# Triangular solves of a chunked delta rule: the substitution left to one engine, two groups interleaved, blocks moved by transfers

## The chip, the cores and the metric

The kernel runs on one NeuronCore of a Trainium2 chip. The metric is the device time of one execution in microseconds (us), taken as the median of several runs. Five engines work in parallel, each in its own program order: PE (TensorE: matrix products, with PEld for its weight loads), DVE (VectorE), ACT (ScalarE), POOL (GpSimd) and SP (SyncE, which here only issues transfers). Engines wait for each other by semaphores. SBUF is the on-chip memory of 128 rows, and PSUM takes the products of TensorE.

## The reference

Three parts follow each other. The first is a linear attention with a delta rule, for 4 batches, 8 heads, 768 tokens and head size 48; the other two are a gated block and a mixer block of dense products.

```python
k_n = k / (norm(k) + 1e-6)
for t in range(S):
    y[t]  = q[t] @ state
    v_old = state.T @ k_n[t]
    state = state + beta[t] * outer(k_n[t], v[t] - v_old)
# then
h = gelu(x @ w_in); u, v = halves of h; v = layernorm(v)*g_ln
x = x + (u * (w_sg @ v + b_sg)) @ w_out
u = x + (relu(x.T @ w_tok1) @ w_tok2).T
out = u + relu(u @ w_ch1) @ w_ch2
```

The change concerns the first part alone.

## The kernel before

The attention goes over six groups, g = 0 to 5. A group is two batches by 256 tokens, and holds four steps c = 0 to 3 of 64 tokens each, for all eight heads. Inside 64 tokens the recurrence is replaced by the inverse T of a triangular matrix, which is worked out per group ahead of time, so that the recurrence over the tokens becomes a recurrence over c.

The preparation of one group (`prep`, `qk`) has these parts:

- kk: the products K K^T (line 141 on TensorE), four blocks per group in a PSUM tile `gm`. ScalarE moves each block out in pieces of 32 rows: four copies to `Md` (line 145, the 32 by 32 diagonal blocks) and two to `G` (line 146, the blocks below them).
- pre: VectorE transposes `Md` to `Li` (line 151), works out the norms and scales `Li` (lines 158 to 170).
- solve: 31 steps of forward substitution on 128 rows at once (128 rows by 8 problems each). Step j takes a product `p` (line 191) and adds it to `T` (line 193). The columns of T are cut into three sets: columns 0 to 3 and 4 to 10 or 11 go to VectorE, and the rest to GpSimd; each set has its own `p`.
- post: four transposes of 32 rows (line 197) put T^T in its place in `tw`, the operand of the chain, and one of 128 rows (line 201) makes `Tn`.
- merge and wt: products on TensorE (lines 209, 218, 229) join two 32-token blocks to one of 64 and multiply with K; ScalarE takes each out of PSUM (lines 212, 221, 232).
- qk: the products Q K^T (line 121), four blocks per group. VectorE multiplies each by a triangular mask into `aq` (line 128), two instructions per block; for group 0 ScalarE copies and GpSimd masks.
- V: GpSimd scales all of V by the norms (line 91), and ScalarE copies it to its place in `yr` for each c (line 238, `vput`).

The recurrence of a group (`chain`) is a generator of 16 slots, four per c: `u` (products ck, line 270, and four copies, line 272), `d0` (products Sps, line 256, and copies, line 258; V of the next c), `y0` and `y1` (output products, line 246). Between the slots a table, `act`, lists what of the preparation of groups g+1 and g+2 is issued there: K a block of kk, Q one of qk, S n steps of the solve, m a merge, w a wt, l and v the loading and placing of V. In the last slots of `chain` of group 5 the dense part begins (`tail`).

The order of the work is written out by hand: there is no scheduler, each engine runs its instructions in the order in which the Python code issues them, and a transfer stands in the order of the engine that issues it. `warm(n)` issues n products on a tile of zeros (line 300, into `wm`), whose results nobody reads. Beside the chains of groups 1 and 2 `beside` converts a weight (lines 413 to 418 on VectorE, 389 and 391 on GpSimd, its transfers on SP).

## Time and profile before

| | |
|---|---|
| median of 3 runs | 1005.87 us (1003.7 to 1007.04) |
| span of the profiled execution | 1010.4 us |
| PE busy | 889.8 us (88%) |
| DVE busy | 660.8 us (65%) |
| ACT busy | 425.5 us (42%) |
| POOL busy | 317.1 us (31%) |

The page gives the span of the profiled execution, from its first to its last instruction, and no other time for it; it lies 4.5 us above the median of the runs. A row of a timeline gives start, duration, engine, line, operation, output and inputs, shape and count; brackets hold how long the engine sat idle before and who ended that. A row of the windows gives a stretch of the span, its length, the busy time of each engine with its instructions, the clock that TensorE was granted as a share of full speed, and the load of the transfer engines. The six chains begin, by their first ck products, at 71, 132, 191.7, 243.8, 290.9 and 325.9 us; the dense part is alone from about 372 us.

### The profile page before, as it was taken

The numbers are of one execution on the slowest core, as the hardware profiler recorded it, in microseconds if no ns is written. First come the engines' busy times: TensorE is split into PE (matmuls) and PEld (weight loads), VectorE is DVE, ScalarE is ACT, GpSimd is POOL, SyncE is SP. The second block draws the span as 40 slices with busy tenths as digits, with TensorE's granted clock in tenths as the row PEclk, the third lists the DMA queues.
The fourth block names the chain that finished last, engine by engine and source line by source line (L and its number), as shares of the span: only waits on it lengthen the run. The fifth ranks groups of instructions, "written<-read, shape, count | busy, mean of one in ns | idle before, by whom it ended". The sixth has DMA issues, their size and how long they took to land.

```text
span 1010.4 us, 23691 instructions
## 1 busy us (share of the span) xinstructions
PE 889.8 (88%) x9764; PEld 819.7 (81%) x9764; DVE 660.8 (65%) x1612; ACT 425.5 (42%) x1029; POOL 317.1 (31%) x475
## 2 busy tenths in 40 slices
PE   6376787777869889999999997988899999999998
PEld 4164666656757678999999996888899999999998
DVE  5999999999993578884956897878623123123122
ACT  6265675666857864442333423334312112112111
POOL 4474446627261234423423453744300000000000
PEclk8688998888999999999999998989999999999999
DMA  9320254715131332000000022223200000000000
GB/s 371 130 49 1 69 127 159 180 57 121 35 75 38 139 125 64 1 1 1 1 2 1 1 72 66 94 63 111 67 24 25 1 24 24 1 24 24 1 25 23
DMA packets 28955, 60.99 MB, mean 60 GB/s; under 512 B 3760, under 2 KB 9904, under 8 KB 28080
## 3 DMA queue, kind: packets, MB, share of 16 engines
q1 hardware_dynamic: 28848, 59.49, 19.1%
q8 instruction: 76, 1.25, 0.5%
q14 instruction: 31, 0.25, 0.1%
HBM read 51.61 MB, written 7.86 MB: 59 GB/s over the span
## 4 chain that ended last, share of the span: by engine, by line
PE 59%; DVE 28%; ACT 7%; issue 4%; POOL 1%; DVEq 0%; POOLq 0%; ACTq 0%
PE ps L489 18%; PE ps L490 18%; PE ps L491 18%; DVE p L191 6%; DVE T L193 6%; DVE tw L197 3%; DVE F L413 2%; DVE aq L128 2%; DVE F L414 2%; PE wm L300 1%; PE ps L513 1%; DVE F L415 1%; DVE F L418 1%; ACT Md L145 1%; DVE Li L151 1%
## 5 line engine op out<-in xcount | busy, mean ns | idle before, releaser
L581 DVE SCALAR_TENSOR_TENSOR hlo<-ps,hh 128x384 fp32r<-128x384 f32 x96 | 53.5, 557 | 208.9 <-ACT hh L580 208.9
L580 ACT ACTIVATE hh<-ps 128x384 fp32r<-128x384 f32 x96 | 47.2, 492 | 229.8 <-PE ps L491 229.8
L489 PE MATMUL ps<-GU,SB 128*128 128x384 f32 x288 | 98.7, 343 | 0.0
L491 PE MATMUL ps<-GU,SB 128*128 128x384 f32 x288 | 98.4, 342 | 0.0
L490 PE MATMUL ps<-GU,SB 128*128 128x384 f32 x288 | 98.1, 341 | 0.0
L191 DVE TENSOR_TENSOR p<-Li,T 128x31 f32<-128x31 f32 (+28 forms) x348 | 87.7, 285 | 1.1
L193 DVE TENSOR_TENSOR T<-T,p 128x31 f32<-128x31 f32 (+28 forms) x348 | 84.1, 274 | 0.8
L490 PE MATMUL ps<-SB,VHt 128*128 128x384 f32 x192 | 65.8, 343 | 2.3 <-POOL SB L391 2.3
L491 PE MATMUL ps<-VHt,hlo 128*128 128x384 f32 x192 | 65.3, 340 | 1.3 <-DVE hlo L581 1.3
L300 PE MATMUL wm<-dum 128*128 128x512 bf16 x156 | 51.5, 436 | 16.4 <-DVE dum L319 14.8
L489 PE MATMUL ps<-SB,VHt 128*128 128x384 f32 x192 | 65.6, 341 | 0.0
L491 PE MATMUL ps<-SB,VHt 128*128 128x384 f32 x192 | 65.2, 339 | 0.0
L489 PE MATMUL ps<-VHt,hh 128*128 128x384 f32 x192 | 65.0, 338 | 0.0
L490 PE MATMUL ps<-VHt,hh 128*128 128x384 f32 x192 | 64.6, 337 | 0.0
L556 POOL TENSOR_TENSOR q<-q,u 128x384 f32<-128x384 f32 x32 | 36.9, 1159 | 66.5 <-DVE q L555 66.5
L489 PE MATMUL ps<-X,SA 128*128 128x384 f32 x144 | 50.0, 347 | 7.2 <-DVE xn L568 3.2
L490 PEld LDWEIGHTS ps<-GU,SB 128*128 128x128 f32 x288 | 54.9, 191 | 0.6 <-DVE GU L506 0.6
L489 PEld LDWEIGHTS ps<-GU,SB 128*128 128x128 f32 x288 | 55.0, 191 | 0.5 <-DVE GU L506 0.5
L491 PEld LDWEIGHTS ps<-GU,SB 128*128 128x128 f32 x288 | 54.8, 190 | 0.3 <-POOL SB L391 0.3
L191 POOL TENSOR_TENSOR p<-Li,T 128x19 f32<-128x19 f32 (+19 forms) x115 | 41.4, 360 | 35.2 <-DVE T L168 27.1
L229 PE MATMUL gm<-tw,kn 128*48 128x64 f32 x768 | 30.2, 245 | 23.9 <-DVE aq L128 19.7
L490 PE MATMUL ps<-X,SA 128*128 128x384 f32 x144 | 49.3, 343 | 0.0
(153 smaller groups left out, 2429.7 us busy)
## 6 DMA issues: line engine op xcount, KB each, us to landing
st<-in_ch_dram SPq DMA_DIRECT2D x36, 256.0 KB, 2.9
kq<-in_kq_dram SPq DMA_DIRECT2D x16, 544.0 KB, 6.8
v<-in_vn_dram SPq DMA_DIRECT2D x12, 384.0 KB, 4.2
out_dram<-xn SPq DMA_DIRECT2D x24, 192.0 KB, 1.9
aq<-in_qt_dram SPq DMA_DIRECT2D x4, 1024.0 KB, 14.9
aq<-in_qt_dram SPq DMA_DIRECT2D x8, 512.0 KB, 7.7
kn<-in_kn_dram SPq DMA_DIRECT2D x2, 1536.0 KB, 17.2
st<-in_win_dram SPq DMA_DIRECT2D x12, 256.0 KB, 4.7
```

The source lines that it names most:

```text
L128: else: nc.vector.tensor_tensor(aq[rr,par].rearrange("p a c x -> p (a c) x"),gp[rr],mask[rr].rearrange("p t x -> p (t x)").unsqueeze(1).to ...
L191: e.tensor_tensor(p,Li[:,j,j+1:].unsqueeze(1).to_broadcast([128,w,n]),T[:,a:a+w,j].unsqueeze(2).to_broadcast([128,w,n]),ALU.mult)
L193: e.tensor_tensor(T[:,a:a+w,j+1:],T[:,a:a+w,j+1:],p,ALU.add)
L197: nc.vector.transpose(out=tw[rr,q//2,:,co:co+32].rearrange("p n i -> p i n"),in_=T[rr].rearrange("p c i -> p i c"))
L229: nc.tensor.matmul(wt[D_[par],2*pair+cc,:],KNs[pb][F_[par],bb,par,2*h+cc,pair,:],tw[F_[par],par,16*bb+8*h+2*pair+cc,:],start=True,stop=True)
L300: for i in range(n): nc.tensor.matmul(t,dum[:,0:128],dum,start=True,stop=True)
L489: nc.tensor.matmul(ps,L[0],Rr[0],start=first,stop=False)
L490: nc.tensor.matmul(ps,L[0],Rr[1],start=False,stop=False)
L491: nc.tensor.matmul(ps,L[1],Rr[0],start=False,stop=last)
L556: nc.gpsimd.tensor_tensor(gt,gt,u2[:,d,t],ALU.mult)
L580: nc.scalar.activation(hi,ps,AF.Relu)
L581: nc.vector.scalar_tensor_tensor(lo,ps,0.0,R(hi),op0=ALU.max,op1=ALU.subtract)
```

## The change

- The substitution is on VectorE alone: one `p` and one sum per step over all columns. The solves of two groups are interleaved: at each step of the group that is due, `filler` may issue one instruction of the next group's solve, at a rate of 0.4 before and after the sum, if all kk blocks of that group have been issued.
- The Gram blocks leave PSUM whole: one copy of 128 by 512 on ScalarE to a staging tile `gf`, and for two blocks together six transfers from SBUF to SBUF, on SP's queue, put the pieces into `md` and `G`. For group 0 the pieces are still copied, half by ScalarE and half by VectorE.
- T^T is transposed once, 128 rows at once, into `md` (line 191 of the new code), and four transfers from SBUF to SBUF (line 204) place it in `tw`, when the solve is through and the chain two groups before is over. `Tn` is made as before.
- GpSimd multiplies V by the norms in the place where it is wanted (64 by 192, four instructions per c); the ScalarE copies of V and the scaling ahead of them go.
- `md`, `Li`, `T` and `Tn` have two buffers, `gf` one. K^T is loaded by halves of a group and once more for qk, without the zeros, which are set on chip.
- The masks of group 0 are on VectorE. The transfers of the converted weight are issued by GpSimd in place of SP. Of the products on zeros only the 36 at the start stay.
- The table `act` is another one, with a row per group; for groups 1 to 4 two of the four wt blocks now come in the first two slots of the chain that uses them.

The end of the solve of group 1 on VectorE (p, T and Li, then the transposes) was, before:

```order
L191 TENSOR_TENSOR p_1245<-Li,T 128x4
L191 TENSOR_TENSOR p_1246<-Li,T 128x8
L193 TENSOR_TENSOR T<-T,p_1245 128x4
L193 TENSOR_TENSOR T<-T,p_1246 128x8
L197 STREAM_TRANSPOSE tw_99<-T 32x32x32 x2
L201 STREAM_TRANSPOSE Tn<-T 128x32x32
L197 STREAM_TRANSPOSE tw_99<-T 32x32x32 x2
L151 STREAM_TRANSPOSE Li<-Md 128x1024
```

and the same place is now (T_147 is group 1's, T_146 group 2's):

```order
L186 TENSOR_TENSOR p_154<-Li_145,T_147 128x60
L188 TENSOR_TENSOR T_146<-T_146,p_153 128x2x30
L188 TENSOR_TENSOR T_147<-T_147,p_154 128x30x2
L126 TENSOR_TENSOR aq_97<-gm,mask 64x512 x2
L186 TENSOR_TENSOR p_154<-Li_145,T_147 128x31
L186 TENSOR_TENSOR p_153<-Li_144,T_146 128x87
L188 TENSOR_TENSOR T_147<-T_147,p_154 128x31
L191 STREAM_TRANSPOSE md_143<-T_147 128x32x32
L194 STREAM_TRANSPOSE Tn_149<-T_147 128x32x32
L188 TENSOR_TENSOR T_146<-T_146,p_153 128x3x29
```

Four transposes of 32 rows became one of 128, and an instruction of the other group stands between some product and its sum.

On SP's queue, in the first chain, there are now the pieces of the Gram blocks and the blocks of T, with none of them before:

```order
L65 DMA kq_110<-in_kq_dram 64x2x512 x2
L152 DMA md_142<-gf 32x2x256
L153 DMA G_128<-gf 32x2x256
L152 DMA md_142<-gf 32x2x256 x2
L153 DMA G_128<-gf 32x2x256
L152 DMA md_142<-gf 32x2x256
L65 DMA kq_111<-in_kq_dram 64x2x512 x2
L204 DMA tw_99<-md_143 32x32x32 x4
```

The T blocks of group 1 (tw_99) stand behind a load of K^T, and the merge products of group 1 wait for them.

On TensorE, around the first merge products of group 1 (tw_99 with G) in the chain of group 0, the row was, before:

```order
L300 LDWEIGHTS dum
L300 MATMUL wm<-dum 128x512
L218 MATMUL gm<-XZ,Tn 32x32 x32
L300 LDWEIGHTS dum
L300 MATMUL wm<-dum 128x512
L209 MATMUL gm<-tw_99,G_140 32x32 x32
L270 MATMUL ck<-yr_104,tw_98 64x48 x8
L270 MATMUL ck<-yr_107,tw_98 64x48 x8
L300 LDWEIGHTS dum
L300 MATMUL wm<-dum 128x512
```

and is now:

```order
L279 MATMUL ck<-yr_104,tw_98 64x48 x8
L279 MATMUL ck<-yr_107,tw_98 64x48 x8
L122 MATMUL gm<-aq_97,kq_111 64x64 x16
L265 MATMUL Sps<-yr_104,kn_100 48x48 x8
L216 MATMUL gm<-tw_99,G_129 32x32 x32
L255 MATMUL yp<-yr_104,aq_96 64x48
```

The products on zeros (wm) are gone there, and the qk products stand ahead of the merge.

The diff, cut to its core:

```diff
-        def scale_v(g):
-            for bb in range(2):
-                nc.gpsimd.tensor_tensor(VS[bb],VS[bb],NN[g][:,16*bb:16*bb+16].unsqueeze(2).to_broadcast([128,16,48]),ALU.mult)
...
+        def kk(g):
+            for u in range(4):
+                h,bb=u//2,u%2; u0=16*bb+8*h
+                kq=take_kq('k',g,u)
...
+                if u%2: load_kq()
+                md=MDs[g%2]; G21=G21s[g%2]
+                if g==0:
+                    for r in range(4):
+                        q=slice(32*r,32*r+32); cp=(nc.scalar.copy,nc.vector.tensor_copy)[r//2]
+                        cp(md[q,u0:u0+8,:],gp[q,:,32*(r%2):32*(r%2)+32])
+                        if r%2==0: cp(G21[q,u0:u0+8,:],gp[q,:,32:64])
+                else:
+                    if bb==0: gf=P1.tile([128,2,2,8,32],F32,name="gf")
+                    nc.scalar.copy(gf[:,:,bb],gp.rearrange("p n (c i) -> p c n i",i=32))
+                    if bb==1:
+                        for r in range(4):
+                            q=slice(32*r,32*r+32)
+                            nc.sync.dma_start(md[q].rearrange("p (b h n) i -> p h b (n i)",b=2,h=2)[:,h],gf[q,r%2].rearrange("p b n i -> p b (n i)"))
+                            if r%2==0: nc.sync.dma_start(G21[q].rearrange("p (b h n) i -> p h b (n i)",b=2,h=2)[:,h],gf[q,1].rearrange("p b n i -> p b (n i)"))
...
             for j in range(31):
-                n=31-j
...
-                for e,a,w,p in todo:
-                    e.tensor_tensor(p,Li[:,j,j+1:].unsqueeze(1).to_broadcast([128,w,n]),T[:,a:a+w,j].unsqueeze(2).to_broadcast([128,w,n]),ALU.mult)
-                for e,a,w,p in todo:
-                    e.tensor_tensor(T[:,a:a+w,j+1:],T[:,a:a+w,j+1:],p,ALU.add)
-                yield 'solve'
-            def ttr(q):
-                rr=slice(32*q,32*q+32); co=32*(q%2)
-                nc.vector.transpose(out=tw[rr,q//2,:,co:co+32].rearrange("p n i -> p i n"),in_=T[rr].rearrange("p c i -> p i c"))
+                n=31-j; w=j+1
+                p=pp[:,:w*n].rearrange("p (w n) -> p w n",n=n)
+                nc.vector.tensor_tensor(p,Li[:,j,j+1:].unsqueeze(1).to_broadcast([128,w,n]),T[:,:w,j].unsqueeze(2).to_broadcast([128,w,n]),ALU.mult)
+                yield 'a'
+                nc.vector.tensor_tensor(T[:,:w,j+1:],T[:,:w,j+1:],p,ALU.add)
+                yield 'b'
+            nc.vector.transpose(out=MDs[s].rearrange("p n i -> p i n"),in_=T.rearrange("p c i -> p i c"))
+            solved[g]=1; tload()
+            yield 'post'
...
+        def tload():
+            for g in range(6):
+                if solved[g] and not loaded[g] and over[0]>=g-2:
+                    loaded[g]=1; tw=TWs[g%2]
+                    for q in range(4):
+                        rr=slice(32*q,32*q+32)
+                        co=32*(q%2); nc.sync.dma_start(tw[rr,q//2,:,co:co+32],MDs[g%2][rr])
...
-                    nc.scalar.copy(YRs[bb][gc%3][T_[par],:,par,:],VS[bb][T_[par],8*h+cc:8*h+cc+7:2,:])
+                    n0=8*h+cc; nc.gpsimd.tensor_tensor(YRs[bb][gc%3][T_[par],:,par,:],VS[bb][T_[par],n0:n0+7:2,:],NNs[g%3][T_[par],16*bb+n0:16*bb+n0+7:2].unsqueeze(2).to_broadcast([64,4,48]),ALU.mult)
...
+        def filler():
+            if len(run)>1 and done[run[1][0]]==4:
+                acc[0]+=rate
+                if acc[0]>=1: acc[0]-=1; next(run[1][1],None)
+        def adv(n):
+            for _ in range(n):
+                if not run: return
+                x=next(run[0][1],None)
+                while x is None and len(run)>1: run.pop(0); x=next(run[0][1],None)
+                if x=='a':
+                    filler(); next(run[0][1]); filler()
...
-                    for x,y in zip(out(r),w): nc.sync.dma_start(x,R(y))
+                    for x,y in zip(out(r),w): nc.gpsimd.dma_start(x,R(y))
...
+_mid=['m z S3','m S3','S3','S3','S3','Q S3','Q S3','Q S3','Q S3','l m S2','m S2','m S2','m K S2','m K S2','m K S2','K v S2']
+ACT=[['S4 K','S4 K','S4 K','S4 K','S4','Q S4','Q S4','Q S4','Q S4','l m S2','m S2','m S2','m K S2','m K S2','m K S2','K v S2'],
+     _c(_mid,(2,6,10,14)),_c(_mid,(2,6,10)),_mid,_mid,['m','m']+['']*14]
+ACT[4]=['m z S4','m S4','S4','S4','S4','Q S4','Q S4','Q m S4','Q m S4','l m S2','m S2','m','m','m','m','v']
+CFG={'nl':(0.5,0.2,0.7),'cg':2,'k0':(2,5,8,11),'rate':.4,'act':ACT}
```

In the new table, S n advances the solve by n steps (a step is a product and its sum), m is one step of merge or wt, and c a step of the weight's conversion.

More of the change, by code (lines that the diff above doesn't have):

```diff
@@ new lines, in kk, with solve @@
+                done[g]+=1
+                yield 'kk'
+        done=[0]*6; merged=[0]*6; loaded=[0]*6; solved=[0]*6
+        def solve(g):
+            s=g%2; Li=Lis[s]; T=Ts[s]; pp=PP[s]
+            assert done[g]==4
+            if g>1: nc.gpsimd.memset(T,0.0)
+            nc.vector.transpose(out=Li,in_=MDs[s].rearrange("p n i -> p i n"))
+            yield 'li'
+            Tf=T.rearrange("p i j -> p (i j)")
+            n2=Li.rearrange("p i j -> p (i j)")[:,0:1024:33]
+            sh,rc,bi=[P2.tile([128,32],F32,name=x) for x in ('sh','rc','bi')]; s1,nr,rr2=rc,sh,rc
+            nc.scalar.activation(sh,n2,AF.Sqrt)
@@ L203, in prep, with zero @@
             yield 'post'
+        over=[-1]
+        def tload():
[5 more added lines that the diff above has]
+                        co=32*(q%2); nc.sync.dma_start(tw[rr,q//2,:,co:co+32],MDs[g%2][rr])
+        def zero(g):
+            tw=TWs[g%2]
+            for par in range(2): nc.gpsimd.memset(tw[D_[par],par,:,0:32],0.0)
@@ L308, in until_, with seqs, many @@
-        def until_(it,kind,n=1): return until(it,kind,n)
-        nd=cfg.get('nd',0)
-        preps={0:prep(0)}; qks={0:qk(0)}
-        p0=preps[0]
+        def seqs(*its):
+            for it in its:
+                for x in it: yield x
+        def many(it,n):
+            for _ in range(n):
+                if next(it,None) is None: return
+        kks=seqs(*(kk(g) for g in range(6))); qks=seqs(*(qk(g) for g in range(6))); ms=seqs(*(merge(g) for g in range(6)))
+        run=[(g,solve(g)) for g in range(1,6)]; acc=[0.0]; rate=cfg['rate']
@@ L314, in phase_a @@
-        until(p0,'pre',2)
-        preps[1]=prep(1)
+        many(kks,4)
+        s0=solve(0)
+        many(s0,4)
+        load_b(1)
         for ns in range(31):
-            until(p0,'solve')
-            if ns%4==2 and ns<16: until(preps[1],'kk')
-            if ns==cfg.get('wj',18): nc.vector.memset(dum[:,0:2],0.0); warm(cfg.get('wu',24))
-        for i in range(2):
-            for k in range(2): nc.scalar.copy(TWs[1][:,i,16*k:16*k+16],XZ.rearrange("p t a b -> p (t a b)").rearrange("p (a b) -> p a b",b=64))
@@ L336, in phase_a @@
+            many(s0,2)
+            if ns in cfg['k0']: many(kks,1)
+            if ns==cfg.get('wj',18): nc.vector.memset(dum[:,0:2],0.0); warm(cfg.get('wu',22))
+        many(s0,1)
+        for k_ in range(4):
+            many(s0,1)
+            many(qks,1)
+        many(ms,1); adv(1)
+        many(ms,1)
+        for k_ in range(6): many(ms,1); adv(1)
+        vput(0,0)
+        act=cfg['act']
         for g in range(6):
-            if g+1<6: qks[g+1]=qk(g+1)
-            if g+2<6: preps[g+2]=prep(g+2)
+            if g+2<6: load_b(g+2)
```

252 lines of the change are left out of this document (97 added, 155 removed).

## The prediction

> **What bounds the kernel now.** I read the slices of the page first, to find where TensorE isn't the bound.
>
> ```profile
> PE   6376787777869889999999997988899999999998
> DVE  5999999999993578884956897878623123123122
> PEclk8688998888999999999999998989999999999999
> ```
>
> A slice is 25.3 us. From slice 2 to 12 VectorE shows 9 throughout while TensorE shows 3 to 8; after slice 15 TensorE is the bound, and nothing of the change lies there. The windows, cut at the first ck products of each chain, give the same in numbers.
>
> ```profile
> 0.00:71.00 71.00, 40.33 (x813) 28.84 (x813) 57.65 (x161) 35.81 (x82) 36.97 (x70) 0.78 0.49 188
> 71.00:132.00 61.00, 43.91 (x1050) 34.46 (x1051) 58.79 (x206) 34.99 (x95) 31.07 (x76) 0.87 0.21 53
> 132.00:191.70 59.70, 43.17 (x1048) 36.42 (x1048) 58.80 (x178) 37.88 (x103) 33.31 (x67) 0.85 0.52 143
> 191.70:243.80 52.10, 40.34 (x1019) 33.09 (x1017) 49.44 (x155) 34.04 (x93) 23.53 (x50) 0.89 0.44 107
> 243.80:290.90 47.10, 38.58 (x1050) 32.13 (x1050) 44.85 (x142) 33.99 (x92) 22.21 (x48) 0.95 0.17 46
> 290.90:325.90 35.00, 31.32 (x919) 26.07 (x918) 21.03 (x58) 25.59 (x67) 7.81 (x11) 1.00 0.34 78
> 372.00:1011.00 639.00, 613.52 (x3415) 597.50 (x3413) 342.68 (x670) 189.29 (x421) 148.33 (x140) 0.98 0.10 33
> ```
>
> The third busy time is VectorE's: 211.9 of 219.9 us in chains 0 to 3. In chain 4 it has 21 of 35 and is no longer the bound. So a microsecond off VectorE before 291 us is worth up to a microsecond, until another engine takes over; chain 4's 35 us show how short a chain can be. The last 639 us stay as they are. VectorE's time up to 325.9 us is 290.6 us, and these groups carry it:
>
> ```profile
> L191 DVE TENSOR_TENSOR p<-Li,T 128x31 f32<-128x31 f32 (+28 forms) x348 | 87.7, 285 | 1.1
> L193 DVE TENSOR_TENSOR T<-T,p 128x31 f32<-128x31 f32 (+28 forms) x348 | 84.1, 274 | 0.8
> L197 DVE STREAM_TRANSPOSE tw<-T 32x1024 f32<-32x1024 f32 x24 | 47.3, 1971 | 0.9
> L128 DVE TENSOR_TENSOR aq<-gm,mask 64x512 f32<-64x512 f32 x40 | 27.6, 689 | 15.0 <-PE gm L121 14.1
> L201 DVE STREAM_TRANSPOSE Tn<-T 128x1024 f32<-128x1024 f32 x6 | 11.9, 1990 | 0.2
> L151 DVE STREAM_TRANSPOSE Li<-Md 128x1024 f32<-128x1024 f32 x6 | 11.8, 1972 | 9.6 <-ACT Md L145 9.4
> ```
>
> A transpose costs the same for 32 rows as for 128.
>
> **Transposes.** 24 of 1.971 us go, 47.3 us; six of 128 rows come at L201's price, 11.9 us: -35.4 us.
>
> **Substitution.** The old instructions overlap, so their durations can't be summed; starts can be subtracted.
>
> ```profile
> 64.73 0.19 DVE L191 TENSOR_TENSOR p<-Li,T 128x31 f32<-128x31 f32 x1
> 64.95 0.19 DVE L193 TENSOR_TENSOR T<-T,p 128x31 f32<-128x31 f32 x1
> 109.69 0.27 DVE L193 TENSOR_TENSOR T<-T,p 128x112 f32<-128x112 f32 x1
> 110.00 0.37 DVE L191 TENSOR_TENSOR p<-Li,T 128x108 f32<-128x108 f32 x2
> 110.31 0.37 DVE L193 TENSOR_TENSOR T<-T,p 128x108 f32<-128x108 f32 x2
> 76.15 0.61 DVE L191 TENSOR_TENSOR p<-Li,T 128x84 f32<-128x84 f32 x2
> 76.68 0.63 DVE L193 TENSOR_TENSOR T<-T,p 128x84 f32<-128x84 f32 x2
> ...
> 76.51 0.47 POOL L193 TENSOR_TENSOR T<-T,p 128x91 f32<-128x91 f32 x1
> 113.49 1.48 POOL L91 TENSOR_TENSOR v<-v,nn 128x768 f32<-128x768 f32 x1 [4.54 <-DMA v<-in_vn_dram]
> ```
>
> An instruction that needs the one ahead of it starts 0.22 us after it at 31 elements and 0.31 at 112: 0.185 us plus 1.05 ns an element. Two that don't need each other (110.00, 135 elements in both) take 0.31 together, 0.085 each plus the same rate. A solve now has 62 instructions over 2 x 5456 elements: 62 x 0.185 + 11.5 = 23.0 us, six of them 138. By the order of instructions 52 of the 372 have the other group's instruction ahead of them and save 0.1 each: 133 us. Before, 290.6 less the transposes (71.0), masks (27.6), the scaling of Li and small steps (25), the weight's conversion (19) and memsets (5) leaves 143. So the solve alone gains 10 us: it does GpSimd's share too, in half the instructions. But at 76 us a pair takes 0.53 us while GpSimd multiplies too, against 0.31 beside no such work: an instruction of GpSimd of 0.47 holds VectorE for some 0.2. Placing V brings 96 such instructions of 64 by 192; GpSimd's 768 elements took 1.48 us, so about 0.5 each. They cost VectorE between 0 and 48 us; at four tenths of their time, for the half of the time that it spends in the solve, 10 us. Net 0, ends -10 and +38.
>
> **Masks, copies, start.** Eight masks of group 0 come to VectorE, 8 x 0.69 = +5.5 us. Its twelve copies of group 0's blocks and the new memsets lie in the time that it waits for `Md` (L151, 9.4 us). After the first solve 2 us of transpose and 5.5 of masks stand where 7.9 of transposes stood, and the four T transfers take the place of the last two transposes. Chain 0 starts at about 71 as before.
>
> So VectorE's work falls by 30 us (35.4 - 5.5). ScalarE loses the V copies and 24 pieces a group for 4 copies, which hide as it isn't the bound.
>
> **New waits.** (1) The next group's Li transpose stands in VectorE's order inside the solve ahead of it, and now waits for kk, ScalarE's copy and six transfers: TensorE's last kk stands at the end of the chain. From the order VectorE gets there first at the end of chain 0, by about 6 us; later it arrives last. Behind it stands the rest of solve 2. I take +6, ends 0 and 15. (2) The T transfers.
>
> ```profile
> bt<-in_bt_dram SPq DMA_DIRECT2D x6, 16.0 KB, 6.6
> scr<-sh SPq DMA_DIRECT2D x12, 128.0 KB, 3.2
> q1 hardware_dynamic: 28848, 59.49, 19.1%
> ```
>
> No row shows SBUF to SBUF. One T transfer has 128 KB as `scr` has (3.2 us), but in pieces of 128 bytes: 4096 for four, 256 per transfer engine. At the queue's mean packet time, 19.1% x 16 x 1010.4 / 28848 = 0.107 us for 2 KB, that is 27 us; bounds 3 and 27. Short pieces are nearer to the bytes, so 8. The order ends the solves of groups 2 to 5 six or more slots ahead of their merge, which covers that; only group 1 (two slots) waits, while VectorE goes on with solve 2. [...] (3) SP's queue has ten more transfers per chain half; behind them stand loads wanted a chain later. The weight's 36 transfers on GpSimd stand ahead of V, which has about eight slots to spare.
>
> **The end.** VectorE's last transposes were over at 306.6 (302.68 + 3.96, below); now 306.6 - 30 + 6 = 282.6. The order lets TensorE merge group 4 from the third mask of chain 3, some 16 us of VectorE's work ahead of that: 266.6. Then come slots 9 to 15 and chain 4.
>
> ```profile
> 302.68 3.96 DVE L197 STREAM_TRANSPOSE tw<-T 32x1024 f32<-32x1024 f32 x2
> ...
> 290.88 0.26 PE L270 MATMUL ck<-yr,tw 128*64 128x48 f32 x1
> 298.84 0.22 PE L209 MATMUL gm<-tw,G 128*32 128x32 f32 x2 [0.26 <-DVE tw L197]
> 300.77 1.17 PE L209 MATMUL gm<-tw,G 128*32 128x32 f32 x62 [1.72 <-DVE tw L197]
> 325.88 0.26 PE L270 MATMUL ck<-yr,tw 128*64 128x48 f32 x1
> L300 PE MATMUL wm<-dum x112: 376/389/634, 73.2 to 323.1; 128*128 128x512 bf16 x112
> L238 ACT COPY yr<-v 64x192 f32<-64x192 f32 x85 | 29.7, 350 | 1.7
> ```
>
> Slots 9 to 15 took 25 us with eight merge and wt steps, four qk, products on zeros and V copies. In chain 3 now two wt and four qk are elsewhere: about 14, so chain 4 begins at 280.6. Chain 4 took 35; less the 1.7 wait for a transpose, five us of products on zeros and half of 16 V copies of 0.35, plus two wt: 27.5. Chain 5 begins at 308 in place of 325.9: -17.8. The profiled 1010.4 become 992.6; the median lies 4.5 under its profile, so **988 us**.
>
> **Rivals.** *VectorE's gain in full, and more*: GpSimd's V costs nothing, the Li wait is hidden, TensorE keeps up. Then -30 - 10 and 5 us more where chain 4 needn't wait: -45, 961 us. For it: 14.1 us of waits in L128 that could shrink too. Against: the alternation at 76 us.
>
> *TensorE's clock falls* (the slower side). 112 products on zeros in the chains go, 112 x 0.33 = 37 us of activity.
>
> ```profile
> 287.19 1.95 PE L229 MATMUL gm<-tw,kn 128*48 128x64 f32 x32 [5.10 <-DVE aq L128]
> 323.42 1.10 PE L229 MATMUL gm<-tw,kn 128*48 128x64 f32 x32
> ```
>
> After 5.1 us idle the same 32 products take 1.95 us, not 1.10: a factor of 1.77. Chains 0 to 4 have 39.5 us of TensorE each, 32 without the zeros. If half of that ran slow, 12 us a chain more, two thirds of it in the slots where VectorE or the next mask waits: 8 x 5 = 40, 1028 us. It decides once over 4 us a chain lies on the path. For: the granted clock is only 0.85 to 0.89 with the zeros. Against: merges, copies and ck alternate closely, and VectorE's own work covers much. [...]
>
> *T's short pieces are dear*: 27 us in place of 8. Chain 0 starts 19 us later, group 1's merge 19 later with some 13 covered by solve 2: +25, 1013 us.
>
> *The interleaving does nothing*: the order fills 52 of 372 gaps, worth 5 us; this only shifts the forecast to 993.
>
> **How the numbers follow.** Forecast with its own spread (968 to 1003) 0.58; gain in full 0.16; clock 0.14; T's pieces 0.08; VectorE's gain eaten by waits for V or masks, no change, 0.04. I call a change under 0.3% (3 us) none. Faster: 0.56 of the forecast's, 0.16 of the full gain, 0.01 of T's = 0.73; same: 0.02 of the forecast's, 0.03 of T's, 0.03 of the last = 0.08; slower: 0.14 of the clock's, 0.04 of T's, 0.01 of the last = 0.19. The range reaches down to the gain in full and up between T's price and the clock's: 957 to 1018.
>
> **What would show it.** Right: chain 5's first ck at about 308; VectorE busy some 260 us until then; the transpose groups at 36 us; adds 0.3 us apart at 112 elements; Li idle for transfers under 10 us. Clock below 0.8 in chains 0 to 3 speaks for the clock rival; merge products idle over 10 us for transfers at two chains, for T's pieces. It is wrong if chains 1 to 3 stay above 52 us with VectorE under 90% busy, or if GpSimd's V products hold VectorE longer than they last.

## The result and the profile after

The changed kernel takes 1053.59 us (median of 4 runs, 1051.51 to 1054.81), the kernel before 1006.38 us: 1.047 times as long, with an interval of 1.0451 to 1.049. Forecast were 988 us. The change is 47 us slower where it was to be 18 us faster.

The slices of the page, now 26.2 us each:

```profile
PE   6375455755566998999999999789999999999998
DVE  7977919969584247887494789786942222222222
PEclk7588678866778899999999999898999999999999
```

From slice 2 to 12 VectorE showed 9 throughout; now it has a 1, a 5 and a 6 there, and TensorE shows 3 to 7. Neither is busy all the time: the chains wait. The windows, cut again at the first ck products of each chain (third busy time VectorE, then ScalarE and GpSimd):

```profile
0.00:76.17 76.17, 42.07 (x805) 31.27 (x806) 61.82 (x129) 16.18 (x34) 30.23 (x42) 0.73 0.59 133
76.17:141.99 65.82, 39.08 (x1095) 37.20 (x1092) 47.61 (x116) 21.91 (x54) 11.33 (x19) 0.79 0.34 79
141.99:203.64 61.65, 36.46 (x1030) 34.32 (x1026) 46.97 (x115) 24.51 (x61) 17.29 (x30) 0.78 0.56 142
203.64:269.92 66.28, 37.37 (x989) 35.52 (x991) 54.73 (x122) 25.36 (x63) 34.83 (x62) 0.69 0.54 139
269.92:327.57 57.65, 34.09 (x902) 31.96 (x898) 40.68 (x89) 21.70 (x54) 14.28 (x25) 0.73 0.43 104
327.57:366.52 38.95, 30.01 (x965) 28.59 (x963) 6.51 (x9) 21.87 (x55) 6.58 (x14) 0.87 0.40 84
```

Until chain 5 VectorE is busy for 258.3 us against 290.6 before: 32 us of work are gone, as forecast. But it is idle for 108.2 us (366.5 less 258.3) against 35.3 (325.9 less 290.6). Chain 5 begins 40.6 us later than before. That is the whole of the difference between the two profiles (1049.8 against 1010.4, 39.4 us): behind it the changed kernel takes 683.3 us, the kernel before 684.5. Between the medians it is 47 us, because the profile of before lies 4 us above its median and this one 4 us below. VectorE's groups, and ScalarE's copy to `gf`:

```profile
L186 DVE TENSOR_TENSOR p<-Li,T 128x31 f32<-128x31 f32 (+15 forms) x186 | 71.2, 385 | 5.6
L188 DVE TENSOR_TENSOR T<-T,p 128x112 f32<-128x112 f32 (+15 forms) x186 | 69.4, 375 | 5.8
L126 DVE TENSOR_TENSOR aq<-gm,mask 64x512 f32<-64x512 f32 x48 | 33.1, 689 | 21.7 <-PE gm L122 20.8
L191 DVE STREAM_TRANSPOSE md<-T 128x1024 f32<-128x1024 f32 x6 | 12.3, 2054 | 0.2
L148 ACT COPY gf<-gm 128x512 f32<-128x512 f32 x20 | 11.6, 583 | 38.6 <-DMA md<-gf 36.8 <-PE gm L138 1.6
L194 DVE STREAM_TRANSPOSE Tn<-T 128x1024 f32<-128x1024 f32 x6 | 11.5, 1923 | 0.0
L161 DVE STREAM_TRANSPOSE Li<-md 128x1024 f32<-128x1024 f32 x6 | 11.5, 1917 | 43.5 <-DMA md<-gf 43.5
```

The last number is the idle time just ahead of the group. The transposes cost what was forecast. What is new stands in the last row, 43.5 us in which VectorE waits for the Gram blocks' transfers, and in the row of `gf`. The waits between 70 and 360 us (total, times, longest) show who waits along:

```profile
DVE Li L161 <- DMA md<-gf: 43.5, 4, 21.2
...
ACT sh L166 <- DVE Li L161: 30.2, 4, 8.1
ACT gf L148 <- DMA md<-gf: 30.0, 4, 8.7
...
PE gm L216 <- DMA tw<-md: 8.9, 2, 7.1
```

The first three can be followed where chain 0 passes into chain 1, in a timeline of four engines (SPq is SP's queue: start and length of the issue):

```profile
137.02 0.64 SPq L152 DMA_DIRECT2D md<-gf  x1
...
141.06 0.59 SPq L152 DMA_DIRECT2D md<-gf  x1
...
146.27 0.58 ACT L148 COPY gf<-gm 128x512 f32<-128x512 f32 x1 [7.88 <-DMA md<-gf]
...
148.78 0.64 SPq L152 DMA_DIRECT2D md<-gf  x1
...
152.05 0.59 SPq L152 DMA_DIRECT2D md<-gf  x1
...
154.62 1.19 SPq L76 DMA_DIRECT2D aq<-in_qt_dram  x2
...
154.20 1.90 DVE L161 STREAM_TRANSPOSE Li<-md 128x1024 f32<-128x1024 f32 x1 [21.21 <-DMA md<-gf]
...
156.14 0.26 ACT L166 ACTIVATE sh<-Li 128x32 f32<-128x32 f32 x1 [7.38 <-DVE Li L161]
...
163.41 1.06 PE L122 MATMUL gm<-aq,kq 128*64 128x64 f32 x29 [0.18 <-DMA aq<-in_qt_dram]
```

Two blocks of group 3 are in `gf`; SP issues six transfers from 137.02 to 141.65. ScalarE has the third block to copy, but `gf` has one buffer: it stands for 7.88 us until the transfers have landed, and so does everything that ScalarE has to do for the chain behind it. Then six more transfers, to 152.64. VectorE has reached the next group's `Li` 21.21 us before these land, in the midst of the solve ahead, and the rest of that solve stands behind. ScalarE's square root stands behind `Li`, the chain's copies behind that. And only at 154.62 does SP get to the next Q load, so that the first Q product on it comes at 163.41.

### The profile page after: what moved, and what is told of

Its sections match the earlier page's. It is cut to its first block, busy times and chain, and to the rows that moved or that the text cites. A ratio compares the mean times of both kernels' runs of the same rounds, so it can differ in the third digit from the quotient of the medians.

```text
span 1049.8 us, 23037 instructions
## 1 busy us (share of the span) xinstructions
PE 872.0 (83%) x9644; PEld 827.4 (79%) x9644; DVE 627.5 (60%) x1294; ACT 350.7 (33%) x809; POOL 282.5 (27%) x358
## 3 DMA queue, kind: packets, MB, share of 16 engines
q1 hardware_dynamic: 57808, 60.28, 21.8%
## 4 chain that ended last, share of the span: by engine, by line
PE 60%; DVE 18%; ACT 7%; DMA 5%; issue 5%; SPq 4%; POOL 1%; DVEq 0%; ACTq 0%; POOLq 0%
PE ps L488 17%; PE ps L489 17%; PE ps L490 17%; DVE T L188 3%; DVE p L186 2%; DMA md<-gf 2%; DVE F L412 2%; DMA aq<-in_qt_dram 2%; DVE F L413 2%; PE gm L122 2%; PE gm L226 2%; SPq L152 2%; DVE aq L126 1%; PE gm L216 1%; PE ps L512 1%
## 5 line engine op out<-in xcount | busy, mean ns | idle before, releaser
L247 POOL TENSOR_TENSOR yr<-v,nn 64x192 f32<-64x192 f32 x96 | 50.9, 530 | 161.4 <-PE yp L255 84.8
L186 DVE TENSOR_TENSOR p<-Li,T 128x31 f32<-128x31 f32 (+15 forms) x186 | 71.2, 385 | 5.6
L122 PE MATMUL gm<-aq,kq 128*64 128x64 f32 x768 | 39.2, 270 | 41.0 <-issue 26.2
L188 DVE TENSOR_TENSOR T<-T,p 128x112 f32<-128x112 f32 (+15 forms) x186 | 69.4, 375 | 5.8
L122 PEld LDWEIGHTS gm<-aq,kq 128*64 128x64 f32 x768 | 35.7, 182 | 43.5 <-issue 35.6
L489 PE MATMUL ps<-SB,VHt 128*128 128x384 f32 x192 | 65.6, 342 | 2.3 <-POOL SB L390 2.3
L488 PE MATMUL ps<-SB,VHt 128*128 128x384 f32 x192 | 65.6, 341 | 0.0
L488 PE MATMUL ps<-X,SA 128*128 128x384 f32 x144 | 50.0, 347 | 5.6 <-DVE xn L567 3.1
L265 PE MATMUL Sps<-yr,kn 128*48 128x48 f32 x704 | 31.6, 232 | 27.1 <-ACT yr L281 13.8
```

Source lines behind the costliest of these rows:

```text
L122: nc.tensor.matmul(gp[T_[par],n,:],kq[F_,par,64*n:64*n+64],aq[F_,par,n//2,n%2,:],start=True,stop=True)
L186: nc.vector.tensor_tensor(p,Li[:,j,j+1:].unsqueeze(1).to_broadcast([128,w,n]),T[:,:w,j].unsqueeze(2).to_broadcast([128,w,n]),ALU.mult)
L188: nc.vector.tensor_tensor(T[:,:w,j+1:],T[:,:w,j+1:],p,ALU.add)
L247: n0=8*h+cc; nc.gpsimd.tensor_tensor(YRs[bb][gc%3][T_[par],:,par,:],VS[bb][T_[par],n0:n0+7:2,:],NNs[g%3][T_[par],16*bb+n0:16*bb+n0+7:2].un ...
L265: nc.tensor.matmul(Sps[bb][D_[par],pair,:],KNs[pb][F_,bb,par,c,pair,:],yr[F_,pair,par,:],start=(gc==0 and pair==0 and bb==0),stop=True,ski ...
L488: nc.tensor.matmul(ps,L[0],Rr[0],start=first,stop=False)
```

## The experiments

Theories. **Staging**: the Gram transfers hold the chains, by `Li` and its square root that wait in their engines' orders, by the one `gf`, and by the loads that stand behind on SP. **Clock** (the prediction's rival on the slower side): without the products on zeros TensorE's clock falls. Later, another question: why does VectorE's lighter load bring nothing even where the waits are gone?

Ratios are to the kernel before on the same chip, with 95% intervals. "Chain 5" is its first ck product in the one profiled execution of each kernel (good to some 5 us, as the 4.5 us between the profile of before and its runs show; e8_r0_q_pc was profiled in its fastest execution, 5 us under its median), and VectorE's busy and idle time is until then. Diffs are cut to their core.

| kernel | us | ratio | chain 5 | VectorE busy | idle |
|---|---|---|---|---|---|
| before | 1006.4 | 1 | 325.9 | 290.6 | 35.3 |
| changed | 1053.6 | 1.0451 to 1.049 | 366.5 | 258.3 | 108.2 |
| e3_zeros | 1062.1 | 1.0507 to 1.0576 | 377.7 | 258.0 | 119.7 |
| b2_nozeros | 1004.6 | 0.9964 to 1.0002 | 320.5 | 289.2 | 31.3 |
| e1_gf2 | 1039.9 | 1.0285 to 1.0358 | 355.5 | 259.5 | 96.1 |
| e2_qpool | 1056.6 | 1.0418 to 1.0556 | 372.7 | 255.9 | 116.8 |
| e4_pieces | 1026.9 | 1.007 to 1.0313 | 341.8 | 259.7 | 82.2 |
| e6_qfirst | 1012.2 | 1.0036 to 1.0074 | 328.3 | 259.9 | 68.5 |
| e5_rate0 | 1025.6 | 1.0128 to 1.0246 | 339.7 | 268.4 | 71.3 |
| e7_r0_q | 1018.3 | 1.0071 to 1.0139 | 331.7 | 268.5 | 63.2 |
| e8_r0_q_pc | 1009.5 | 1.0003 to 1.0053 | 320.2 | 269.0 | 51.2 |
| e9_start | 1008.7 | 0.9977 to 1.0037 | 320.1 | 266.8 | 53.3 |
| e10_cut | 999.1 | 0.9884 to 0.9943 | 315.9 | 244.4 | 71.5 |
| b1_t_dma | 1010.7 | 1.0024 to 1.0064 | 329.0 | 255.6 | 73.4 |
| b3_cut | 985.5 | 0.9759 to 0.9813 | 299.5 | 265.7 | 33.8 |
| b4_tfree | 987.1 | 0.9776 to 0.9825 | 304.1 | 258.2 | 45.9 |
| b5_hybrid | 999.8 | 0.9902 to 0.9947 | 316.3 | 279.1 | 37.3 |
| b6_hyb_nz | 999.1 | 0.9884 to 0.9933 | 312.8 | 278.5 | 34.3 |
| b7_alone | 1010.7 | 1.0016 to 1.0051 | 324.7 | 281.7 | 43.0 |
| b8_alone_hyb | 998.7 | 0.9878 to 0.9946 | 313.7 | 269.2 | 44.5 |

Names with e are variants of the changed kernel, with b of the kernel before. Expectations that speak of 360 us for chain 5 in the changed kernel mean the last ck products of its chain 4; the first of chain 5 come at 366.5.

### The clock

Products on zeros put back into the changed kernel:

```diff
-        act=cfg['act']
+        act=cfg['act']; mc=[8]
+                else: warm(((4,0,1,1,0,0,0,1,2,0,0,2,0,0,1,0) if g==0 else (0,1,0,2,0,0,0,0,2,0,0,0,0,0,1,0))[si])
-                    if a=='K': many(kks,n_)
+                    if a=='K': warm(1); many(kks,n_)
-                    if a=='m': many(ms,n_)
+                    if a=='m': warm(3 if mc[0]%8<4 else 0); mc[0]+=1; many(ms,n_)
```

> The 112 products on zeros (0.33 us each) return to chains 0 to 4 at the places that the kernel before had them; the rest is the changed kernel. Clock theory: granted clock back to 0.85 to 0.95 in chains 0 to 4, time 1010 to 1025. Staging theory: the clock rises somewhat but the waits for md and for the next Q load stay, time 1045 to 1060, Li's waits for md still above 30 us.

Measured 1062.1 us, 8.5 slower than without them. The granted clock was 0.75, 0.84, 0.80, 0.82 and 0.88 in chains 0 to 4, against 0.79, 0.78, 0.69, 0.73 and 0.87: up in four of five, and no time came of it. The edit put 122 products back, ten more than the kernel before has, and in chains 0 to 3 the clock stayed under the 0.85 to 0.95 that was expected, so this run alone doesn't settle it.

The same question from the other side, the kernel before with no zeros in its chains:

```diff
-'dk': 1, 'dq': 0, 'dm': 3,
+'dk': 0, 'dq': 0, 'dm': 0, 'burst': {},
...
-'nds': [0, 1, 0, 2, 0, 0, 0, 0, 2, 0, 0, 0, 0, 0, 1, 0]
+'nds': [0]*16
```

> The kernel before without its 112 products on zeros in chains 0 to 4, nothing else changed. Clock theory: the granted clock falls from 0.85 to 0.95 to under 0.8 in these chains and the time rises by 20 to 45 us, 1026 to 1051. Staging theory: VectorE's order sets the length of the chains and covers it, 995 to 1012.

Measured 1004.6 us, ratio 0.9983: no loss. The mean clock to chain 5 went from 0.87 to 0.85. So the products on zeros weren't missed, neither here nor there. With its waits undone and still no products on zeros (e8_r0_q_pc, below) the changed kernel's clock is 0.81 to 0.91 in chains 0 to 4, against 0.69 to 0.87: the low clock went with the waits.

### The Gram transfers

Two buffers for `gf`:

```diff
-        MDs,Lis,Ts,TNs=[[P1.tile([128,32,32],F32,name=f"{n_}{i}") for i in range(2)] for n_ in ('md','Li','T','Tn')]
+        MDs,Lis,Ts=[[P1.tile([128,32,32],F32,name=f"{n_}{i}") for i in range(2)] for n_ in ('md','Li','T')]
+        TNs=[P1.tile([128,32,32],F32,name="Tn")]*2
...
-                    if bb==0: gf=P1.tile([128,2,2,8,32],F32,name="gf")
+                    if bb==0: gf=P1.tile([128,2,2,8,32],F32,name=f"gf{h}")
```

> Two buffers for gf in place of one (the transposed T has one buffer in place of two, to make room). The third copy of a group no longer waits for the first six transfers to land (30.0 us in four waits). Staging theory: a gain of 10 to 25 us, 1029 to 1044, less what the single buffer of the transposed T costs (it is read by merge one chain later; under 5). Clock theory: no change, 1051 to 1056.

Measured 1039.9 us, 13.7 less than the changed kernel, inside the staging theory's 10 to 25. The one buffer is part of the loss, not most of it.

The Q load from GpSimd's queue:

```diff
-                nc.sync.dma_start(aq[H_[par],:,:,par].rearrange("p h b x -> p (h b) x"),I['qt'][bp,sc][H_[par]].rearrange("p h b x -> p (h b) x"))
+                (nc.sync if g<2 else nc.gpsimd).dma_start(aq[H_[par],:,:,par].rearrange("p h b x -> p (h b) x"),I['qt'][bp,sc][H_[par]].rearrange("p h b x -> p (h b) x"))
```

> Only the Q load of groups 2 to 5 changes: GpSimd issues it in place of SP, so it no longer stands behind six Gram transfers (about 4 us of issue) and what they wait for. Staging theory: the first mask of chains 1 to 4 comes 4 to 8 us earlier, but Li and Sqrt still stand behind md: a gain of 5 to 20 us, 1034 to 1049. Clock theory: no change, 1051 to 1056.

Measured 1056.6 us, no gain, as the clock theory had it. But the run doesn't tell the theories apart: the load now made GpSimd wait until its tile was free, and V's products stood behind. The waits of this run:

```profile
POOL aq L76 <- PE yp L255: 25.5, 3, 9.3
```

Blocks in six ScalarE pieces for every group, so without these transfers:

```diff
-                if g==0:
+                if True:
...
-cp=(nc.scalar.copy,nc.vector.tensor_copy)[r//2]
+cp=(nc.scalar.copy,nc.vector.tensor_copy if g==0 else nc.scalar.copy)[r//2]
```

> The Gram blocks of every group leave PSUM in six pieces straight to md and G, on ScalarE for groups 1 to 5, as before the change; the 12 transfers per group and the tile gf go, everything else of the change stays. Staging theory (the 60 transfers, 0.6 us each to issue on SP, one gf buffer, and Li, its Sqrt on ScalarE and the next Q load standing in order behind them, hold chains 1 to 4): most of the 47 us comes back, chain 5's first ck from 360 to about 325, time 1005 to 1020, Li's waits for md fall from 43.5 us to under 15. Clock theory (112 products on zeros are gone, the granted clock of 0.70 to 0.78 stretches TensorE's part of each chain): the products on zeros stay away, so the time stays at 1045 to 1055 and the clock below 0.8.

Measured 1026.9 us (two runs, 1021.8 and 1031.9): 27 us come back with no product on zeros. That speaks for staging, but the median is 7 us above the top of its range. What was left showed in the waits of this run:

```profile
DVE Li L161 <- ACT md L144: 11.2, 1, 11.2
...
PE gm L122 <- DMA aq<-in_qt_dram: 10.6, 5, 5.7
DVE bi L177 <- DMA bt<-in_bt_dram: 10.2, 2, 7.9
```

Beta and Q come late, both loaded on SP behind T's transfers and the K load.

### The order of the loads

Q ahead of T and K, beta's six loads at the start:

```diff
-            if g+2<6: load_b(g+2)
-            if g+1<6 and g>0: load_q(g+1)
...
-            over[0]=g; tload()
+            if g+2<6: load_q(g+2)
+            over[0]=g; tload()
```

> The variant with the Gram blocks in six pieces (1026.9 us), and on SP the next Q load issued ahead of T's transfers and the K load, the six beta loads all at the start in tiles of their own. In the run without this VectorE idled 17.2 us in chain 4 until the products on the late Q, 10.2 us for beta, and TensorE waited 10.6 us for Q. If the order of the loads behind each chain's end is the second part of the loss: 1003 to 1017. If these waits only stand in for VectorE's own order: 1022 to 1030.

Measured 1012.2 us, 14.7 less than with the pieces alone, inside the 1003 to 1017. Even so it is slower than before (1.0036 to 1.0074).

### The interleaving

The changed kernel with its transfers, and no interleaving:

```diff
-'rate':.4
+'rate':0.0
```

> The changed kernel with the interleaving off: no step of the next group's solve stands among those of the solve under way, so the Li transpose that waits for md and its Sqrt on ScalarE stand at the end of the solve ahead. Staging theory: Li's waits (43.5 us) shrink to under 25, the solve ahead ends sooner, 1030 to 1048. If the interleaving is worth what the order's 52 filled gaps say (5 us) and Li's place costs nothing: 1055 to 1062.

Measured 1025.6 us, 28 less than the changed kernel, and below the 1030 that the staging theory had as its best. VectorE's work got longer (268.4 against 258.3, most of it in the substitution: 148.3 against 140.6), and its idle time fell from 108.2 to 71.3. The `Li` followed above (154.20) now stands behind the solve ahead and its transposes, and waits for nothing; its row in this run's timeline:

```profile
166.00 1.81 DVE L161 STREAM_TRANSPOSE Li<-md 128x1024 f32<-128x1024 f32 x1
```

This with the loads' order as above (and one buffer for `p`, to make room):

> The changed kernel with the interleaving off and, on SP, the next Q load ahead of T's transfers and the K load, beta's six loads at the start (as in the two runs before, 1025.6 and, with six pieces, 1012.2 us); the Gram transfers stay. If the interleaving (Li and its Sqrt standing early in their engines' orders, waiting for md) and the place of the Q load are two separate losses: 1025.6 less 10 to 16, 1008 to 1016. If the Q load's wait is only what the Gram transfers make of it and goes with them: 1022 to 1028.

Measured 1018.3 us, 7.3 less. It is 2 us above the range for two separate losses and 4 below that for one. With the pieces and the interleaving the order of the loads was worth 14.7. Both differences start from a kernel with two runs, and the ratios' intervals overlap in both, so that it is worth less here isn't shown.

And with the six pieces as well:

> The run above with the Gram blocks in six ScalarE pieces as well, so no transfers from gf. If the transfers cost time only through the Li that waits for them in the midst of a solve, this equals the run above within 4 us. If they cost time by their own place too (six of 0.6 us on SP ahead of K, Q and T, G's landing): 6 to 15 us less, 996 to 1006, which would be at or below the kernel before.

Measured 1009.5 us, another 8.8 us less (expected: 6 to 15, if the transfers cost time by their own place). So from the changed kernel: interleaving -28.0, loads' order -7.3, transfers -8.8, together -44.1 of the 47 us. Undone in the other order the same 44.1 are transfers -26.7 (e4_pieces), loads' order -14.7 (e6_qfirst), interleaving -2.7. Each of the two, the interleaving and the transfers, is worth 27 to 28 us while the other is there, and 3 to 9 when it is gone: most of the loss is what they do together, an `Li` that waits for transfers in the midst of another solve. With six pieces the interleaving costs little or nothing (1012.2 with it, 1009.5 without, intervals that overlap), though one `Li` still waits 13 us for ScalarE's copies there.

Without the interleaving another wait grows. The square root stands in ScalarE's order ahead of the chain's copies, and `Li` now comes behind a whole solve. Rows of the waits, e6_qfirst first, then e8_r0_q_pc:

```profile
DVE Li L161 <- ACT md L144: 13.0, 1, 13.0
ACT sh L166 <- DVE Li L161: 8.2, 4, 2.2
...
ACT sh L166 <- DVE Li L161: 49.9, 4, 16.2
```

Between 70 us and chain 5 it is 10.7 us in three waits in the kernel before. No run moved the square root, so what it still costs is open; as e6_qfirst, where it waits 8.2 us, is no faster, the rest isn't this wait alone.

### The start

```diff
-        for par in range(2): nc.vector.memset(AQs[0][T_[par],:,:,par].rearrange("p h b a c x -> p (h b) (a c x)"),0.0)
...
         many(kks,4)
+        for par in range(2):
+            for h in range(2):
+                for bb in range(2): nc.scalar.copy(AQs[0][T_[par],h,bb,par].rearrange("p a c x -> p (a c x)"),XZ[T_[par],0].rearrange("p a b -> p (a b)"))
```

> The run above, and the zeros of the first aq are written by ScalarE behind its first copies in place of two VectorE memsets of 1.76 us that stood ahead of VectorE's copies of group 0. Li of group 0 was 4.9 us later than in the kernel before (21.29 against 16.40), and chain 0 began 5 to 6 us later. If these memsets are the cause: chain 0 from about 77 to 73, 3 to 5 us less than the run above. If GpSimd's memsets beside the first solve are the cause: no change.

Measured 1008.7 us, no difference that can be told. `Li` of group 0 came at 15.64 in place of 20.84 us, but chain 0 only 2.1 us earlier (75.06 against 77.16). So the memsets were not the whole cause; where part of the 5 us stayed is told in the last section.

### Why VectorE's gain brings nothing

T by one transpose and four transfers, alone, in the kernel before:

```diff
-            ttr(0); ttr(2)
+            Tr=P1.tile([128,32,32],F32,name="Tr")
+            nc.vector.transpose(out=Tr.rearrange("p n i -> p i n"),in_=T.rearrange("p c i -> p i c"))
+            for q in range(4): nc.sync.dma_start(tw[32*q:32*q+32,q//2,:,32*(q%2):32*(q%2)+32],Tr[32*q:32*q+32])
...
-            ttr(1); ttr(3)
```

> One part alone, put into the kernel before: T leaves by one transpose of 128 rows and four transfers from SP's queue in place of four transposes of 32 rows (24 transposes of 1.97 us become 6; unused columns of kq and p make room for the tile). All else is the kernel before, so no Gram transfers, no interleaving, V by ScalarE. Staging theory (the loss comes from the Gram transfers, the single gf and the loads' order, not from T's transfers): VectorE's work up to chain 5 falls by about 35 us, chains 0 to 3 shorten by 4 to 7 us each, 980 to 995. If T's transfers are dear (their landing stands ahead of every merge): 1005 to 1030. Clock theory: the products on zeros are still there, so a gain as well.

Measured 1010.7 us, 0.4% slower, where a gain was expected: VectorE has 35 us less to do and 38 us more idle time until chain 5. Either its time was covered, or the landing of T takes the gain back. Three runs tell this. First, 25 us of VectorE's substitution left out:

```diff
+                if g and 13<=j<18: yield 'solve'; continue
```

> The kernel before with five of the 31 substitution steps (13 to 17) of groups 1 to 5 left out, VectorE's share and GpSimd's: four VectorE instructions a step, about 1.2 us, some 30 us of VectorE in all (and as much of GpSimd); the output is not the reference's. If a microsecond off VectorE before chain 5 is worth up to one (the prediction's premise): 20 to 30 us less, 977 to 988. If it is covered by other engines' waits there: 998 to 1008.

Measured 985.5 us: 21.7 us for 24.9 us of VectorE, 0.87 for one. VectorE did set the time (GpSimd lost 18 us of the same steps, which no run took away alone). Second, T by one transpose without the landing, here against the run with the four transfers:

```diff
-            for q in range(4): nc.sync.dma_start(tw[32*q:32*q+32,q//2,:,32*(q%2):32*(q%2)+32],Tr[32*q:32*q+32])
+            for q in (0,2): nc.vector.tensor_copy(tw[32*q:32*q+32,q//2,0,0:32],Tr[32*q:32*q+32,0])
```

> The kernel before with T by one transpose of 128 rows and no transfers: in their place VectorE copies one block of 32 columns to two of the quadrants, so that merge still waits for VectorE but for no landing; the rest of T isn't placed and the output is not the reference's. The run with the four transfers was 1010.7 (+0.4%), with 30 us less work on VectorE and 31 us more idle. If the landing of T (2 us of transpose, then 4 to 6 us of issue and landing ahead of the merge, where the kernel before starts the merge after the first two transposes) takes the gain back: 980 to 992. If VectorE's time was covered anyway: 1000 to 1008.

Measured 987.1 us, 23.6 less than with the transfers. So the landing takes the gain back. Third, only the quadrants that nobody wants at once go by transfer (against the same run):

```diff
+            ttr(0); ttr(2)
             Tr=P1.tile([128,32,32],F32,name="Tr")
...
-            for q in range(4): nc.sync.dma_start(tw[32*q:32*q+32,q//2,:,32*(q%2):32*(q%2)+32],Tr[32*q:32*q+32])
+            for q in (1,3): nc.sync.dma_start(tw[32*q:32*q+32,q//2,:,32:64],Tr[32*q:32*q+32])
```

> The kernel before with T's two quadrants that merge reads first (0 and 2) by VectorE's transposes as before, then one transpose of 128 rows and two transfers for quadrants 1 and 3, which only the products behind the merge read: five transposes a group become four... the landing of these two lies beside the merge. If the landing was what took the gain back: VectorE falls by 2 us a group, 12 in all, with nothing put back, 996 to 1003. If VectorE's time is covered: 1004 to 1010.

Measured 999.8 us, ratio 0.9925: faster than the kernel before, with 11.5 us less on VectorE and 2 us more idle. The timelines for T of group 5 show it; with four transfers (b1_t_dma):

```profile
293.96 2.10 DVE L199 STREAM_TRANSPOSE Tr<-T 128x1024 f32<-128x1024 f32 x1
...
315.77 1.39 DVE L128 TENSOR_TENSOR aq<-gm,mask 64x512 f32<-64x512 f32 x2 [17.94 <-PE gm L121]
...
299.49 0.22 PE L210 MATMUL gm<-tw,G 128*32 128x32 f32 x2 [3.71 <-DMA tw<-Tr]
301.96 1.88 PE L210 MATMUL gm<-tw,G 128*32 128x32 f32 x62 [2.26 <-DMA tw<-Tr]
```

and with two transposes ahead (b5_hybrid):

```profile
286.44 3.98 DVE L197 STREAM_TRANSPOSE tw<-T 32x1024 f32<-32x1024 f32 x2
...
303.12 1.39 DVE L128 TENSOR_TENSOR aq<-gm,mask 64x512 f32<-64x512 f32 x2 [8.82 <-PE gm L121]
...
290.56 1.14 PE L211 MATMUL gm<-tw,G 128*32 128x32 f32 x61 [0.80 <-DVE tw L197]
```

From the end of the solve to the merge's products it takes 8.0 us with four transfers (293.96 to 301.96) and 4.1 with two transposes (286.44 to 290.56). Before it took the same 4.05 (296.72 to 300.77, the prediction's rows of the end): the merge needs two of the four quadrants, and the two other transposes (302.68) ran beside it. To the next mask it is 21.8 us against 16.7.

Without the products on zeros as well:

> The run above without the 112 products on zeros as well, which by themselves gave 1004.6 against 1007.2 (ratio 0.998). If both gains stand side by side: 2 to 3 us under the run above, 993 to 1001. Clock theory (already against the earlier run): 1015 or more.

Measured 999.1 us, ratio 0.9908: the same as with them, within the interval.

The substitution on VectorE alone, in the kernel before:

```diff
-'bd': (11, 12)
+'bd': (32, 32), 'd0': 32
```

> One part alone, put into the kernel before: the substitution on VectorE alone, one product and one addition per step (62 instructions a solve), GpSimd's share with them; T's transposes, V and all else as before. The prediction's step (133 us for six solves against 143): VectorE loses 5 to 10 us, 998 to 1003. From the changed kernel without interleaving (VectorE's work to chain 5 269 us against 290.6, where the transposes and masks alone make -30): the substitution costs 8 us more, of it some by V on GpSimd; without V 0 to 8 more, 1007 to 1014.

Measured 1010.7 us, 0.33% slower: the rival's range, not the prediction's. The groups tell why:

```profile
L191 DVE TENSOR_TENSOR p<-Li,T 128x31 f32<-128x31 f32 (+15 forms) x186 | 70.5, 379 | 6.0
L193 DVE TENSOR_TENSOR T<-T,p 128x31 f32<-128x31 f32 (+15 forms) x186 | 67.9, 365 | 6.4
```

VectorE is busy for 8.9 us less until chain 5, but each instruction now needs the one ahead of it, and 12.4 us of gaps stand before them (before: 1.1 and 0.8). A solve takes (138.4 + 12.4)/6 = 25.1 us, not 23.0.

> The run with T's two late quadrants by transfers and without the products on zeros (999.1), and the substitution on VectorE alone as well. By the prediction's step 5 to 8 under it, 991 to 995; by the rival's 0 to 6 above it, 999 to 1006.

Measured 998.7 us: neither gain nor loss beside 999.1.

Last, the changed kernel with its three losses undone, and part of the substitution left out:

```diff
+                if g and 13<=j<18: yield 'a'; yield 'b'; continue
```

> The changed kernel without interleaving, with six pieces and the Q load first (1009.5), and steps 13 to 17 of the substitution of groups 1 to 5 left out: ten instructions of about 0.45 us a solve, 22 us of VectorE in all; the output is not the reference's. If VectorE still sets the length of its chains (93 to 95% busy in three of them): 12 to 20 us less, 990 to 998. If the loads, the masks that wait for them and chain 4 set it: 0 to 6 less, 1003 to 1010.

Measured 999.1 us: 10.4 us for 24.6 us of VectorE, 0.42 for one (0.3 to 0.6 by the two intervals), between the two cases. VectorE is about half of what sets these chains; its groups in the run that this builds on (e8_r0_q_pc):

```profile
L186 DVE TENSOR_TENSOR p<-Li,T 128x31 f32<-128x31 f32 (+15 forms) x186 | 74.3, 399 | 6.1
L188 DVE TENSOR_TENSOR T<-T,p 128x31 f32<-128x31 f32 (+15 forms) x186 | 73.9, 398 | 6.4
```

148.2 busy and 12.5 of gaps make 160.7, 10 more than in the kernel before with the substitution on VectorE alone (150.8). GpSimd's V products are the likely cause, since this kernel has them and that one has not: in e9_start, beside them (GpSimd from 26.72 to 30.13), the first sum, over 31 elements, takes 0.48 us, against 0.19 in the kernel before (at 22.29). No run took them away alone.

In the profiles chains 0 to 3 of e9_start take 207.6 us against 219.9 before, with 26 us less of VectorE's work there (185.5 against 211.9). So 12 us are gained in these chains; the start (4.1), chain 4 (2.5) and the part behind it (2.2) give 9 of them back.

## Why the prediction was wrong, point by point

**The bound: right.** VectorE set the chains' length before, and a microsecond off it was worth 0.87 (b3_cut).

**Transposes, -35.4 us: right in work, wrong in worth.** L191, L194 and L161 have 35.3 us against 71.0. But "a microsecond off VectorE before 291 us is worth up to a microsecond" was used for instructions of which half ran beside the merge, and in exchange for a landing ahead of it; in the kernel before this exchange gives +0.4%.

**Substitution, 133 us and 10 for V: too low.** Measured, with the gaps, 152.0 interleaved, 160.7 not interleaved, 150.8 without V beside it and not interleaved. The 138 for six solves that are not interleaved were 12.8 short. The 143 of the kernel before, a remainder of rounded terms, were low as well: b7_alone has 138.4 us of substitution and 8.9 us less of VectorE's work, which makes it 147.3 before, and 149.2 with its gaps. So one engine alone gains nothing. Interleaving gains 8.7 us of VectorE (5 forecast); V's 10 were about right, if V makes the difference of 160.7 and 150.8.

**Masks, +5.5: right.** 33.1 against 27.6.

**Start at about 71: wrong by 5.** VectorE's copies of group 0 were to lie in its wait for `Md`; they stood behind its own memsets, and `Li` came at 21.29 in place of 16.40.

**Wait (1), "I take +6, ends 0 and 15": the step that failed.** `Li` waits 43.5 us in four waits (6.1, 21.2, 8.3 and 7.9), and the run without interleaving is 28 us shorter. The place was right ("behind it stands the rest of solve 2"), the size was not. I had reckoned that VectorE would get there first at the end of chain 0 alone and later arrive last; it came first four times. The working names one batch of six transfers, where the order has two in series (copy, six issues, landing, copy of the third block, six issues, landing), as `gf` has one buffer. And the square root on ScalarE, which stands behind `Li` and ahead of the chain's copies (30.2 us of waits), wasn't in the sum at all.

**Wait (2), T at 8 us for group 1 alone: right.** In the changed kernel merge waits 8.9 us for T's transfers in all, at group 1 alone (7.1 and 1.9). In the kernel before, with its later T, the four transfers make the merge wait at four of six groups (b1_t_dma).

**Wait (3), SP's queue at nothing: wrong.** "behind them stand loads wanted a chain later" overlooked that in the new order the qk products stand in slots 5 to 8 in place of 9 to 12, and that beta is wanted early in the next solve. Without the interleaving the order of the loads is worth 7.3 us (with intervals that overlap) and the transfers' own place 8.8.

**Chain 4 at 27.5 us: wrong.** It took 38.9, and still 34.9 with VectorE busy for 5.5 us of it (e6_qfirst). Its length isn't VectorE's; which of its waits sets it was not tried.

**The sum.** By the rows chain 5 was to begin at 308.1 and began at 366.5, 58.4 us later: 5.2 at the start (76.2 against 71), 41.8 in chains 0 to 3 (251.4 against 209.6) and 11.4 in chain 4 (38.9 against 27.5). The other 7 of the 65.6 us between 988 and 1053.6 lie between profiles and medians. In medians 44.1 are the three waits undone one after the other. With them undone (e9_start, whose profile lies at its median) chains 0 to 3 take 207.6 us, the start 75.1 and chain 4 37.5. So the waits account for chains 0 to 3, and start and chain 4, 14 us together, are errors of their own, of which e9_start undid 2 us. That chains 0 to 3 then come out as forecast is in part luck: VectorE is busy for 185.5 of the 207.6 us and idle for 22, against 8 before, and the substitution is dearer than forecast.

**The rivals.** The clock rival had the sign and the wrong mechanism: the products on zeros neither help the changed kernel (1062.1 us with them, 1053.6 without) nor are missed in the old one (1004.6 without, 1006.4 with). That the interleaving could cost time was in no rival; the one on it had it worth nothing. The row at 287.19 is what it was, a burst after 5.1 us of idle time (1.95 us against 1.10), but no run shows that these chains lose their time in such bursts. "Clock below 0.8 in chains 0 to 3 speaks for the clock rival" was a bad sign to name: it came true (0.69 to 0.79), and with the waits undone the clock was 0.81 to 0.90 there without any product on zeros. Two signs of being right came true too, VectorE's work (258.3 us) and the transposes (35.3): they measure work, not waits. The sign that told was the last: chains 1 to 3 took 61.7, 66.3 and 57.7 us, above 52, with VectorE 71 to 83% busy.

## What to carry to other kernels

Work that another engine or a transfer has yet to feed should not stand in the midst of an in-order engine's longest run of work: here, early in the order, it made all behind it wait too (43.5 us at `Li` on VectorE, 30.2 at the square root on ScalarE). It cost 28 us where two rounds of transfers fed it, and little where copies did (1012.2 against 1009.5). Before exchanging instructions for transfers, look at which part of the result is wanted first: transposes whose result is wanted late are worth replacing (0.9925 with two quadrants), those ahead of a waiting product aren't (1.0044 with four). And a microsecond of the bounding engine can be priced by leaving some of its work out: 0.87 in one kernel and some 0.4 in its rewrite.
